# Attention values product: bursts of eight key tiles instead of four, twelve probability buffers, a smaller GpSimd DMA scratch

## The chip, the cores and the metric

The kernel runs on one core of one Trainium2 chip. The metric is the device time of one execution in microseconds (us), the median of several runs. The engines are named as in the profile: PE is TensorE (PEld its weight loads), DVE is VectorE, ACT is ScalarE, POOL is GpSimd, SP is SyncE, which issues the DMA transfers here.

## The reference

One layer is normalised once and then goes two ways, attention over a sliding window and a gating MLP:

```
xn = layernorm(x)                              # x: 2048 x 640
q, k, v = split(xn @ wqkv)                     # 32 heads of width 20
scores = q k^T / sqrt(20), kept where 0 <= query - key < 256
s = concat(softmax(scores) v) @ wo
r = relu(xn @ w1 + b1)                         # 640 -> 1536
g = silu(r * r @ w2 + b2)                      # 1536 -> 640
out = x + s * g
```

All tensors are float32. The window of 256 means that a tile of 128 keys is seen by three tiles of 128 queries: its own and the next two.

## The kernel before, in words

A first stage (to about 140 us of the span) normalises x, transposes it, and makes v for all heads and q, k for the first heads. Products that need the full precision are split into a high and a low part and run as three matmuls.

The middle stage, from about 140 to 770 us, is a loop of 267 steps (`steps`, line 1199). Heads are taken in pairs: 16 pairs `p` (`NP`), each with 16 tiles of queries or keys (`NT`). Step `s` does this, each part for another tile:

- `scores` (line 471): scores of query tile `s`, one matmul for each head of the pair, written to two PSUM tiles `sps`. The pool `pat` holds two such tiles, so the two of the next step reuse those of this one. `maxima` (line 483) has DVE take the row maxima of each.
- `scores_t` (line 512): transposed scores of the key tile nine steps back (`LAG`), both heads, in one PSUM tile `stps` of two banks, of which there is a single one (`ptp`). `exps` (line 523) has ACT write exp of it to a probability tile `p32`, on which POOL zeroes what the mask excludes.
- Every fourth step `max_rows` (line 489) transposes the maxima through columns 384 to 447 of the `stps` tile.
- `fill` (line 1202) puts matmuls of other work, the filler, into the PE queue: q and k of the later heads and the two MLP layers.
- `values` (line 533) is run two steps after the exp of its last key tile (`PLAG`), once in four steps, for four key tiles: the products of the probabilities with v, accumulated in one PSUM bank `ot` (named ops in the profile). The bank has four columns of 128; the outputs of query tile `t` go to column `t // 2 % 4`, and to one of four groups of 32 rows by head and by the parity of `t`. So query tiles 0 and 1 share the rows and column 0 with query tiles 8 and 9. After the burst, ACT copies the two columns that are complete to `osb` (line 552), which goes to DRAM.

PE works in two ways. For all but `values` the array is cut into two halves of 64 rows, and two streams of matmuls run side by side, one per half (`ahead`, `behind`, `both`, lines 438 to 461; the second stream trails the first a little). In `values` all 128 rows are used and the array is cut into four groups of 32 columns. A change between the two is called a turn here.

The order of each engine's work is the order in which the program emits it (a manual schedule). The emission follows a plan: `clock` holds planned times of the two streams, every matmul adds its cost from `COST` (us, line 42), and a burst adds `PV` (1.57) to both. A step has `pace` of planned time (line 1200), the sum of all planned work over the number of steps. In each step, the scores come first, then filler up to 0.4 of the step (`EARLY_FILL`, line 258), then, in a step with a burst, filler up to `PV` before the step's end and the burst, else filler to the step's end:

```
            fill((s + EARLY_FILL) * pace)
            ...
            if e and e[1] % 4 == 3:
                fill((s + 1) * pace - PV)
                values(e[0], e[1] // 4)
            else:
                fill((s + 1) * pace)
```

`fill` emits nothing when the planned clock is past its argument. Other engines' work (`later`, line 583) is emitted once the planned clock has passed its due time; that check is in `fill` too.

The last stage, from about 770 us, is the projection with wo, the gate and the stores.

Of the kernel before, what the change touches and what calls it, by code (L numbers as in the profile page):

```python
# [9 lines left out]
F32 = mybir.dt.float32  # L10
F32R = mybir.dt.float32r
BF16 = mybir.dt.bfloat16
AF = mybir.ActivationFunctionType
ALU = mybir.AluOpType

P = 128
S = 2048
D = 640
# [3 lines left out]
NT = S // P  # L22
KC = D // P
NP = H // 2
NB = 4
BT = S // NB
# [4 lines left out]
HALF = D // 2  # L31
NFH = F // 2 // P
WIDE = 2
FHALF = F // 2
MT = 256
# [5 lines left out]
WARM2 = 10  # L41
COST = {P: 0.067, 2 * P: 0.12, HALF: 0.147, 3 * P: 0.172, BT: 0.23}
SCALE = DH ** -0.5
PV = 1.57
PLAG = 2
NEG = -1.0e30
EPS = 1e-5
SETTLE = 0.45
# [10 lines left out]
def attn_mlp_kernel(ctx: ExitStack, tc, x, wqkv, wo, w1, b1, w2, b2, out):  # L59
    nc = tc.nc  # L60
# [25 lines left out]
    o_d = [dram.tile([NP, P, MT], F32, name=f"o_{g}") for g in range(NB)]  # L86
# [8 lines left out]

    nc.gpsimd.affine_select(mask[:, 0:P], mask[:, 0:P], pattern=[[1, P]], compare_op=ALU.is_gt, fill=NEG, base=0, channel_multiplier=-1)
    nc.gpsimd.affine_select(mask[:, 2 * P:], mask[:, 2 * P:], pattern=[[-1, P]], compare_op=ALU.is_ge, fill=NEG, base=0, channel_multiplier=1)
    mts = [const.tile([P, HP], F32, name=f"mt{j}") for j in range(2)]
# [314 lines left out]
    at2 = ctx.enter_context(tc.tile_pool(name="at2", bufs=2))  # L413
# [4 lines left out]
    def load_v(p):  # L418
        vp = at2.tile([P, NB, 4, 2, VW], F32, tag="vp", name=f"vp_{p}")
        nc.sync.dma_start(vp.rearrange("p b t h w -> p (b t h w)"), v_d[:, p].rearrange("p b n -> p (b n)"))  # L420
        vps[p] = vp

    clock = [0.0, 0.0, 0.0]
# [85 lines left out]
    def pair_tile():  # L509
        return ptp.tile([P, 2, BT], F32, tag="st", name="stps")  # L510
# [10 lines left out]
        return tps, n  # L521

    def exps(p, kb, tps, n):
        p32 = at2.tile([P, 2, 3 * P], F32, tag="p32", bufs=8, name="p32")
        nc.scalar.activation(p32[:, :, :n], tps[:, :, :n], AF.Exp, scale=SCALE)  # L525
        nc.gpsimd.affine_select(p32[:, :, 0:P], p32[:, :, 0:P], pattern=[[0, 2], [1, P]], compare_op=ALU.is_ge, fill=0.0, base=0, channel_multiplier=-1)  # L526
        if n == 3 * P:
            nc.gpsimd.affine_select(p32[:, :, 2 * P:], p32[:, :, 2 * P:], pattern=[[0, 2], [-1, P]], compare_op=ALU.is_gt, fill=0.0, base=0, channel_multiplier=1)  # L528
        pts[p, kb] = p32

    ot = po_.tile([P, 4, P], F32, tag="o", name="ops")

    def values(p, g):
        for kb in range(4 * g, 4 * g + 4):
            pt = pts.pop((p, kb))
            ts = range(kb, min(kb + 3, NT))
            same, other = [t for t in ts if t % 2 == kb % 2], [t for t in ts if t % 2 != kb % 2]
            parts = [same] if kb % 8 < 6 else [[t] for t in same]
            for part in parts + [other]:
                for hh in range(2):  # L540
                    if not part:
                        continue
                    t = part[0]
                    r0 = 32 * (2 * hh + t % 2)
                    c0 = t // 2 % 4
                    first = t % 8 < 2 and kb == max(0, t - 2) or kb == 0
                    nc.tensor.matmul(ot[r0:r0 + VW, c0:c0 + len(part), :], vps[p][:, kb // 4, kb % 4, hh, :], pt[:, hh, :].rearrange("p (t n) -> p t n", n=P)[:, t - kb:part[-1] - kb + 1:2, :], start=first, stop=part[0] == kb, skip_group_check=True)  # L547
        clock[:2] = [max(clock[:2]) + PV] * 2

        def evac():  # L550
            osb = at2.tile([P, 2, P], F32, tag="osb", name="osb")
            nc.scalar.activation(osb, ot[:, 2 * g % 4:2 * g % 4 + 2, :], AF.Copy)
            post(o_d[g][p], osb.rearrange("p e n -> p (e n)"), 0.8)
        later(SOON, evac)


# [4 lines left out]
    def post(dst, src, wait=0.0, then=lambda: None):  # L561
        def go():
            posts.append((dst, src))
            then()
        if whole[0] or not wait:
            go()
        else:
            later(wait, go)

    def post_all():  # L570
        for dst, src in posts:
            nc.sync.dma_start(dst, src)
        posts.clear()
# [9 lines left out]
    def later(wait, fn):  # L583
        tasks.append((clock[0] + wait, len(tasks), fn))

    def soon():
        while tasks:
            first = min(tasks)
            if first[0] > clock[0]:
                return  # L590
            tasks.remove(first)
            first[2]()
# [104 lines left out]
    def ensure_bulk(items):  # L697
        for it in items:
            if it in bulk:
                bulk.remove(it)  # L700
                it[1]()
# [345 lines left out]
    def stored(g):  # L1047
        return NP * NT - NT + 4 * g + 3 + LAG + PLAG

# [19 lines left out]

    def room_of(tag, name):  # L1070
        if tag == "p32":
            return at2.tile([P, 2, 3 * P], F32, tag="p32", bufs=8, name=name).rearrange("p a n -> p (a n)")[:, :D]
        return wgt.tile([P, D], F32, tag=tag, name=name)

    ybt = {}
# [3 lines left out]
    def fetch_y():  # L1079
        if y_early and (1, y_early[0][0]) in stored_y and (y_early[0][2] == 0 or whole[0]):  # L1080
            t, w, i, k = y_early.pop(0)
            if not k:
                y_room.append((at, at1)[i].tile([P, S], F32, tag=f"{w}s{i}", name=f"y{w}{i}"))
            slot = y_room[-1][:, k * D:(k + 1) * D]
            nc.sync.dma_start(slot, y_d[1][:, t, :])
            ybt[t] = slot
# [110 lines left out]

    fl = filler()
    steps = NP * NT + LAG + PLAG
    pace = (8 * (KC - 1) * 15 * COST[BT] + 2 * NB * (15 * (WIDE * COST[BT] + 2 * (NFH - WIDE) * COST[MT]) + 8 * 18 * COST[HALF]) + NP * (2 * NT * COST[3 * P] + NB * PV)) / (steps - 1)  # L1200

    def fill(upto):
        soon()
        while clock[0] < upto:
            c = next(fl, None)
            if c is None:
                clock[0] = upto
                soon()
                return
            if whole[0]:  # L1210
                clock[:2] = [clock[0] + c] * 2
            soon()

    with tc.manual_schedule(engines={E_.PE, E_.Activation, E_.DVE, E_.Pool, E_.SP}):
        load_v(0)
        nc.vector.memset(ot, 0.0)
        loads = []

        def at_step(n):
            return divmod(n, NT) if 0 <= n < NP * NT else None  # L1220

        for s in range(steps):
            state[2] = s
            vload[0] = 0.2 * (s % 4 == 0) + 0.5 * (s % 4 == 3)
            post_all()
            invert()
            if s >= NP * NT - NT + LAG + 2:
                fetch_y()
            issue(RATE)
            a, b, e = (at_step(s - lag) for lag in (0, LAG, LAG + PLAG))  # L1230
            if a:
                p, q = a
                if q == 0:
                    ensure_bulk(loads)
                if s == 2:
                    ones_rows(1)
                if q == 2 and p < NP - 1:
                    assert made_for(p + 1, 0)
                    loads = [bulk_dma(0.7, *l) for l in pair_loads(p + 1, 0)]
                if q == LAG and p < NP - 1:  # L1240
                    assert made_for(p + 1, 1)
                    loads += [bulk_dma(0.7, *l) for l in pair_loads(p + 1, 1)]
                if q == LAG + 4 and p < NP - 1:
                    load_v(p + 1)
            rows = None
            if a:
                sc = scores(p, q)
            if b:
                stp = scores_t(*b)
            if s % 4 == 0 and 0 < s <= NP * NT:  # L1250
                rows = max_rows((s - 1) // NT, (s - 1) % NT // 4, stp[0] if b else pair_tile())
            if a:
                maxima(*a, *sc)
            if b:
                exps(*b, *stp)
            if rows:
                rows()
            fill((s + EARLY_FILL) * pace)
            post_all()
            issue(RATE)  # L1260
            flush()
            tick()
            if e and e[1] % 4 == 3:
                fill((s + 1) * pace - PV)
                values(e[0], e[1] // 4)
            else:
                fill((s + 1) * pace)
        finish()
        post_all()
        state[2] = 10 ** 6  # L1270
        for _ in fl:
            post_all()
            flush(mark() - 1)
        flush()
        post_all()
# [23 lines left out]
```

## Time and profile before

| | |
|---|---|
| median of 3 runs | 851.1 us (851.03 to 851.38) |
| span of the profiled execution, first to last instruction | 849.5 us (the profile lists no other time of this execution) |
| mean granted clock of TensorE | 0.999 |
| PE busy | 841.8 us, 10160 matmuls |
| DVE, ACT, POOL busy | 457.9, 420.9, 330.4 us |
| matmuls of `values` | 2112 instructions in 64 bursts, from 151.8 to 767.7 us |
| copies of their results by ACT | 64 of 378 ns |
| DMA, share of 16 engines (q1, issued by SP) | 63.9%, 164.64 MB |

A busy time is the time in which at least one instruction of the engine runs; those of PE overlap one another. A row of the timeline gives the start, the duration, the engine, the line, the operation, what it writes and reads, the shapes and, in square brackets, how long the engine had been idle and what released it. A float32 matmul of `values` is two instructions in the profile.

### The profile page before, as it was taken

The numbers are of one execution on the slowest core, as the hardware profiler recorded it, in microseconds if no ns is written. First come the engines' busy times: TensorE is split into PE (matmuls) and PEld (weight loads), VectorE is DVE, ScalarE is ACT, GpSimd is POOL, SyncE is SP. The second block draws the span as 40 slices with busy tenths as digits, with TensorE's granted clock in tenths as the row PEclk, the third lists the DMA queues.
The fourth block names the chain that finished last, engine by engine and source line by source line (L and its number), as shares of the span: only waits on it lengthen the run. The fifth ranks groups of instructions, "written<-read, shape, count | busy, mean of one in ns | idle before, by whom it ended". The sixth has DMA issues, their size and how long they took to land.

```text
span 849.5 us, 25542 instructions
## 1 busy us (share of the span) xinstructions
PE 841.8 (99%) x10160; PEld 784.3 (92%) x10160; DVE 457.9 (54%) x1370; ACT 420.9 (50%) x792; POOL 330.4 (39%) x652
## 2 busy tenths in 40 slices
PE   9999999999999999999999999999999999999997
PEld 8999999888888999999999999999999999999997
DVE  7653126665567645455445466755455455436753
ACT  5232114545556763664653664853763754763321
POOL 6010002434334553553552553643553543542442
PEclk9999999999999999999999999999999999999999
DMA  7997587868979565337248245576456355467993
GB/s 248 316 403 286 176 207 260 268 215 266 309 246 288 152 196 151 93 116 200 79 151 219 86 126 151 141 224 188 111 163 199 109 166 190 129 155 212 291 233 118
DMA packets 94398, 166.42 MB, mean 196 GB/s; under 512 B 10952, under 2 KB 43848, under 8 KB 93256
## 3 DMA queue, kind: packets, MB, share of 16 engines
q1 hardware_dynamic: 94120, 164.64, 63.9%
q8 instruction: 80, 1.31, 0.7%
q14 instruction: 38, 0.31, 0.1%
q10 hardware_dynamic: 160, 0.16, 0.1%
HBM read 93.66 MB, written 70.52 MB: 193 GB/s over the span
## 4 chain that ended last, share of the span: by engine, by line
PE 97%; DVE 1%; DMA 1%; issue 0%; ACT 0%; SPq 0%; DVEq 0%
PE yps L469 21%; PE hps L469 21%; PE qkps L469 14%; PE ops L547 10%; PE wops L607 8%; PE vps L229 8%; PE stps L519 5%; PE sps L479 4%; PE qkps L206 3%; PE tps L173 1%; DMA qs<-q_d 0%; DMA xt<-in_A_x_dram 0%; PE tps L302 0%; PE stps L494 0%; PE warm_ps L316 0%
## 5 line engine op out<-in xcount | busy, mean ns | idle before, releaser
L487 DVE CUSTOM_DVE_ANT_0 junk<-sps,mask 128x384 bf16<-128x384 f32 (+2 forms) x512 | 272.6, 532 | 257.7 <-PE hps L469 73.4
L525 ACT ACTIVATE p<-stps 128x768 f32<-128x768 f32 (+2 forms) x256 | 197.4, 771 | 257.2 <-PE stps L519 209.8
L526 POOL TENSOR_SCALAR_AFFINE_SELECT p<-p 128x256 f32<-128x256 f32 x256 | 110.1, 430 | 322.3 <-ACT p L525 317.0
L469 PE MATMUL yps<-w,hh 64*128 64x320 f32 x1536 | 228.3, 310 | 0.8 <-DVE ysb L996 0.7
L469 PE MATMUL hps<-xb,w 64*128 64x256 f32 (+1 forms) x2100 | 218.6, 305 | 0.0
L469 PEld LDWEIGHTS hps<-xb,w 64*128 64x128 f32 x2100 | 199.2, 187 | 6.2 <-issue 5.1
L469 PEld LDWEIGHTS yps<-w,hh 64*128 64x128 f32 x1536 | 181.9, 185 | 5.9 <-issue 3.4
L469 PE MATMUL yps<-w,hl 64*128 64x320 f32 x768 | 174.1, 309 | 0.0
L479 PE MATMUL sps<-ks,qs 60*128 60x384 f32 (+2 forms) x512 | 142.5, 340 | 0.2 <-DVE mt L487 0.2
L519 PE MATMUL stps<-qs,ks 62*128 62x384 f32 (+2 forms) x512 | 136.0, 330 | 0.1
L469 PEld LDWEIGHTS yps<-w,hl 64*128 64x128 f32 x768 | 113.7, 185 | 1.7 <-issue 1.7
L469 PE MATMUL qkps<-xT,wgkh 64*128 64x512 f32 x320 | 100.4, 395 | 0.0
L469 PE MATMUL qkps<-xT,wgqh 64*128 64x512 f32 x320 | 97.8, 392 | 0.0
L528 POOL TENSOR_SCALAR_AFFINE_SELECT p<-p 128x256 f32<-128x256 f32 x224 | 93.6, 418 | 0.0
L547 PE MATMUL ops<-p,vp 128*21 128x128 f32 (+1 forms) x2112 | 92.8, 313 | 0.0
L519 PEld LDWEIGHTS stps<-qs,ks 62*128 62x128 f32 x512 | 88.2, 187 | 1.3 <-issue 0.4
L479 PEld LDWEIGHTS sps<-ks,qs 60*128 60x128 f32 x512 | 86.2, 185 | 2.3 <-DVE mt L487 0.8
L547 PEld LDWEIGHTS ops<-p,vp 128*21 128x21 f32 x2112 | 65.2, 100 | 23.6 <-issue 11.6
L229 PE MATMUL vps<-wv,xT 128*128 128x320 f32 x480 | 71.5, 308 | 0.0
L229 PEld LDWEIGHTS vps<-wv,xT 128*128 128x128 f32 x480 | 70.5, 188 | 0.1
L966 POOL TENSOR_TENSOR hl<-sq,hh 128x512 fp32r<-128x512 f32 x48 | 62.2, 1297 | 18.9 <-ACT sq L965 18.8
L607 PE MATMUL wops<-wo,oT 128*128 128x320 f32 x384 | 61.6, 309 | 0.0
(104 smaller groups left out, 1165.0 us busy)
## 6 DMA issues: line engine op xcount, KB each, us to landing
ks<-k_d SPq DMA_DIRECT2D x64, 240.0 KB
qs<-q_d SPq DMA_DIRECT2D x64, 240.0 KB
xb<-xs SPq DMA_DIRECT2D x60, 256.0 KB
xs<-xT SPq DMA_DIRECT2D x8, 1280.0 KB
k_d<-shm SPq DMA_DIRECT2D x19, 512.0 KB
q_d<-shm SPq DMA_DIRECT2D x19, 512.0 KB
y<-ysb SPq DMA_DIRECT2D x28, 320.0 KB
o<-osb SPq DMA_DIRECT2D x64, 128.0 KB
```

The costliest lines, as they stand in the source:

```text
L206: nc.tensor.matmul(ps, wt[:, c, :], xT[part][b][:, c * BT + t0:c * BT + t0 + n], start=m == 1, stop=m == 3 * KC)
L229: nc.tensor.matmul(ps, xT[xp][b][:, c * BT + t * P: c * BT + (t + 1) * P], wv[wp][:, c, nh * HALF:(nh + 1) * HALF], start=first and m == 0 ...
L469: return nc.tensor.matmul(out, a[r], b_[r], skip_group_check=True, **kw)
L479: nc.tensor.matmul(ss[hh][:, :nk], qs[i][o, q * P:(q + 1) * P], ks[i][o, k0 * P:k0 * P + nk], start=True, stop=True)
L487: nc.vector.tensor_tensor_reduce(out=junk[:, :nk], in0=ss[hh][:, :nk], in1=mask[:, 3 * P - nk:], scale=1.0, scalar=-3.0e38, op0=ALU.add, o ...
L519: nc.tensor.matmul(tps[:, hh, :n], ks[i][o, kb * P:(kb + 1) * P], qs[i][o, kb * P:kb * P + n], start=True, stop=True)
L525: nc.scalar.activation(p32[:, :, :n], tps[:, :, :n], AF.Exp, scale=SCALE)
L526: nc.gpsimd.affine_select(p32[:, :, 0:P], p32[:, :, 0:P], pattern=[[0, 2], [1, P]], compare_op=ALU.is_ge, fill=0.0, base=0, channel_multip ...
L528: nc.gpsimd.affine_select(p32[:, :, 2 * P:], p32[:, :, 2 * P:], pattern=[[0, 2], [-1, P]], compare_op=ALU.is_gt, fill=0.0, base=0, channel ...
L547: nc.tensor.matmul(ot[r0:r0 + VW, c0:c0 + len(part), :], vps[p][:, kb // 4, kb % 4, hh, :], pt[:, hh, :].rearrange("p (t n) -> p t n", n=P ...
L607: nc.tensor.matmul(ps, a, b_, start=j == 0, stop=j == n - 1)
L966: nc.gpsimd.tensor_sub(hh[1][:, :BT], sq, f32(hh[0]))
```

## The change

`values` takes a range of key tiles in place of a group number. For the first 15 head pairs there are two ranges of eight tiles, for the last pair four of four as before. The planned cost of a burst becomes `TURN + PV * len` with 0.33 and 0.31 us, which is 1.57 for four tiles as before and 2.81 for eight. A burst of eight reaches query tile 8, whose column is that of query tiles 0 and 1; so in the burst, after its second key tile, ACT is given a copy of that one column (`leave`, at `kb % 8 == 1`), and the other three are copied after the burst. The probability tiles go from eight buffers to twelve. The DMA scratch that is set aside for GpSimd shrinks to 2048 bytes per partition.

```diff
-PV = 1.57
+PV = 0.31
+TURN = 0.33
+PBUF = 12
...
-        p32 = at2.tile([P, 2, 3 * P], F32, tag="p32", bufs=8, name="p32")
+        p32 = at2.tile([P, 2, 3 * P], F32, tag="p32", bufs=PBUF, name="p32")
...
-    def values(p, g):
-        for kb in range(4 * g, 4 * g + 4):
+    def bursts(p):
+        return (range(0, 8), range(8, NT)) if p < NP - 1 else [range(4 * g, 4 * g + 4) for g in range(NB)]
+
+    def burst_of(p, kb):
+        return next((r for r in bursts(p) if r[-1] == kb), None)
+
+    def burst_cost(r):
+        return TURN + PV * len(r)
+
+    def values(p, kbs):
+        osbs, out_ = {}, set()
+
+        def leave(g, e):
+            if g not in osbs:
+                osbs[g] = at2.tile([P, 2, P], F32, tag="osb", name="osb")
+            nc.scalar.activation(osbs[g][:, e], ot[:, (2 * g + e.start) % 4:(2 * g + e.start) % 4 + e.stop - e.start, :], AF.Copy)
+
+        for kb in kbs:
             pt = pts.pop((p, kb))
...
-        clock[:2] = [max(clock[:2]) + PV] * 2
+            if kb % 8 == 1 and kb + 6 in kbs:
+                leave(kb // 4, slice(0, 1))
+                out_.add(kb // 4)
+        clock[:2] = [max(clock[:2]) + burst_cost(kbs)] * 2
 
         def evac():
-            osb = at2.tile([P, 2, P], F32, tag="osb", name="osb")
-            nc.scalar.activation(osb, ot[:, 2 * g % 4:2 * g % 4 + 2, :], AF.Copy)
-            post(o_d[g][p], osb.rearrange("p e n -> p (e n)"), 0.8)
+            for g in sorted({kb // 4 for kb in kbs}):
+                leave(g, slice(int(g in out_), 2))
+                post(o_d[g][p], osbs[g].rearrange("p e n -> p (e n)"), 0.8)
...
-    pace = (... + NP * (2 * NT * COST[3 * P] + NB * PV)) / (steps - 1)
+    pace = (... + NP * 2 * NT * COST[3 * P] + sum(burst_cost(r) for p in range(NP) for r in bursts(p))) / (steps - 1)
...
-            if e and e[1] % 4 == 3:
-                fill((s + 1) * pace - PV)
-                values(e[0], e[1] // 4)
+            r = e and burst_of(*e)
+            if r:
+                fill((s + 1) * pace - burst_cost(r))
+                values(e[0], r)
...
-    nc = bacc.Bacc("TRN2", target_bir_lowering=False, num_devices=1)
+    nc = bacc.Bacc("TRN2", target_bir_lowering=False, num_devices=1, dynamic_dma_scratch_size=2048)
```

More of the change, by code (lines that the diff above doesn't have):

```diff
@@ L1071, in room_of @@
         if tag == "p32":
-            return at2.tile([P, 2, 3 * P], F32, tag="p32", bufs=8, name=name).rearrange("p a n -> p (a n)")[:, :D]
+            return at2.tile([P, 2, 3 * P], F32, tag="p32", bufs=PBUF, name=name).rearrange("p a n -> p (a n)")[:, :D]
         return wgt.tile([P, D], F32, tag=tag, name=name)
@@ L1199, in attn_mlp_kernel @@
     steps = NP * NT + LAG + PLAG
-    pace = (8 * (KC - 1) * 15 * COST[BT] + 2 * NB * (15 * (WIDE * COST[BT] + 2 * (NFH - WIDE) * COST[MT]) + 8 * 18 * COST[HALF]) + NP * (2 * NT * COST[3 * P] + NB * PV)) / (steps - 1)
+    pace = (8 * (KC - 1) * 15 * COST[BT] + 2 * NB * (15 * (WIDE * COST[BT] + 2 * (NFH - WIDE) * COST[MT]) + 8 * 18 * COST[HALF]) + NP * 2 * NT * COST[3 * P] + sum(burst_cost(r) for p in range(NP) for r in bursts(p))) / (steps - 1)
     def fill(upto):
```

## The prediction

> **What bounds the kernel now.** I read the profile's page first, then PE's own waits.
>
> ```profile
> span 849.5 us, 25542 instructions
> PE 841.8 (99%) x10160; PEld 784.3 (92%) x10160; DVE 457.9 (54%) x1370; ACT 420.9 (50%) x792; POOL 330.4 (39%) x652
> PE 97%; DVE 1%; DMA 1%; issue 0%; ACT 0%; SPq 0%; DVEq 0%
> ...
> PE warm_ps L269 <- POOL ident L92: 1.7, 1, 1.7
> PE yps L469 <- DVE ysb L996: 0.7, 1, 0.7
> PE sps L479 <- DVE mt L487: 0.2, 1, 0.2
> ```
>
> PE carries 97% of the chain of waits and waits 2.6 us in all. So every us of PE work that goes is a us of time, and every new PE wait is one too: there is no slack on PE to hide it. The plan's clock follows the chip well (below), so the question is what the new burst does to PE's work and to PE's waits.
>
> Next the timeline of PE around two bursts (start, duration):
>
> ```profile
> 307.14 0.34 PE L479 MATMUL sps<-ks,qs 60*128 60x384 f32 x1
> 307.37 0.34 PE L479 MATMUL sps<-ks,qs 60*128 60x384 f32 x1
> ...
> 308.26 1.21 PEld L547 LDWEIGHTS ops<-p,vp 128*21 128x21 f32 x32 [0.19 <-issue]
> 308.26 1.50 PE L547 MATMUL ops<-p,vp 128*21 128x256 f32 x32
> ...
> 309.69 0.18 PEld L469 LDWEIGHTS yps<-w,hh 64*128 64x128 f32 x1 [0.22 <-issue]
> 309.70 0.44 PE L479 MATMUL sps<-ks,qs 60*128 60x384 f32 x1
> ...
> 317.51 0.32 PE L469 MATMUL yps<-w,hl 64*128 64x320 f32 x2
> 317.66 0.45 PE L469 MATMUL yps<-w,hh 64*128 64x320 f32 x3
> 318.04 1.52 PE L547 MATMUL ops<-p,vp 128*21 128x256 f32 x40
> ...
> L547 PE MATMUL ops<-p,vp x32: 272/334/395, 308.3 to 309.5; 128*21 128x256 f32 x16, 128*21 128x128 f32 x16
> ...
> L547 PE MATMUL ops<-p,vp 128*21 128x128 f32 x1344 | 88.6, 274 | 0.0
> L547 PE MATMUL ops<-p,vp 128*21 128x256 f32 x768 | 75.1, 382 | 0.0
> ```
>
> The two bursts start 9.78 us apart, 2.45 us a step. The plan says 2.40: its whole work is 638.7 us (339.7 and 110.4 us of filler, 88.1 of scores, 64 bursts of 1.57), over 266 steps. The burst starts 1.12 us after its step's scores; the plan says 0.4 of a step, 0.96, plus up to one matmul. I rely on that match.
>
> **Turns saved.** 64 bursts become 30 of eight and 4 of four, so 30 pairs of turns go; the matmuls stay. What one pair costs: two row matmuls take 0.15 us (317.51 to 317.66), so the three from 317.66 are worth 0.22, the next could start at 317.88, and the burst starts at 318.04: 0.16 lost on entry. On exit the last weight load ends at 308.26 + 1.21 = 309.47 and the next starts at 309.69: at most 0.22 lost, or nothing if the last matmuls only drain. So 0.16 to 0.38. A middle value comes from the two mean durations: 108 ns more for 128 more columns. The 32 instructions (16 of each form) stream 48 such units over four column groups, 12 x 0.108 = 1.30 us, against 1.43 from burst start to the next row matmul: 0.13 on exit. I take 0.16 + 0.13 = 0.29, 30 times: **-8.7 us** (-4.8 to -11.4).
>
> **The copy inside the burst.** `leave` puts an ACT copy of column 0 behind the second key tile. The third key tile writes columns 1 and 2 of the same bank. Does it wait? The nearest case is the exp in steps with transposed maxima, whose matmuls write columns of the `stps` bank that exp does not read. The timeline of one, and the whole run's waits for that line:
>
> ```profile
> 322.18 0.34 PE L519 MATMUL stps<-qs,ks 62*128 62x384 f32 x1
> 322.36 0.22 PE L494 MATMUL stps<-ident,mt 64*64 64x64 f32 x1
> 322.61 0.81 ACT L525 ACTIVATE p<-stps 128x768 f32<-128x768 f32 x1 [1.09 <-PE stps L494]
> ...
> ACT p L525: 38.7, 44
> ...
> L308 ACT ACTIVATE xT<-tps 128x128 fp32r<-128x128 f32 x4 | 1.1, 270 | 0.0
> L552 ACT ACTIVATE osb<-ops 128x256 f32<-128x256 f32 x64 | 24.2, 378 | 0.0
> ...
> 307.93 0.81 ACT L525 ACTIVATE p<-stps 128x768 f32<-128x768 f32 x1 [0.23 <-PE stps L519]
> 308.64 0.62 ACT L965 ACTIVATE sq<-relu 128x512 f32<-128x512 f32 x1
> ...
> L796 ACT ACTIVATE w<-raw 128x640 fp32r<-128x640 f32 x12 | 8.8, 732 | 0.5 <-DMA raw<-in_B_w_dram 0.5
> ```
>
> Exp starts 0.03 us after the transposes end (322.58), not after the scores it reads (322.52); 44 of its waits go to them. The order is kept for the bank, not for the columns. So I expect the third key tile to wait for the copy.
>
> The Trainium skill agrees in its page "PSUM — Partial Sum Buffer", section "PSUM bank collisions raise a hardware error": two engines on one bank and one quadrant of 32 partitions at a time are an error, whatever the columns, so guard by bank and quadrant, not by address. By that rule this wait comes in all 30 bursts; by addresses alone it would come at the seventh key tile only and cost nothing (the second rival).
>
> Price: the first two key tiles are half of the 32 instructions, so the 16th starts about 0.62 into the burst and ends 0.27 later, at 0.89. The copy starts 0.03 later, lasts 0.27 (the 128-column row of line 308), and PE goes on 0.06 after it (DVE to PE, 248.61 to 248.67 in the rows of the next part): 1.25. Without the copy the third tile would start at 0.65. That is 0.60 lost, with PE idle and everything in its queue behind. Below, 0.36 if the drain costs nothing. Above, 1.3 when a weight split of 0.73 stands ahead on ACT; in the burst above exp and the square keep ACT until 1.00, so the copy is 0.08 late. I take 0.60 + 0.06: **+19.8 us** (+11 to +30; the 1.3 can't hold for all).
>
> **The step after the burst.** Before, the plan's clock stood at 0.96 + 1.57 = 2.53 us after a burst: a step and 0.13. Now the pace is 2.364 (628.8 us over 266), 0.4 of it 0.946, and the burst 2.81: 3.756, that is 1.59 steps. `fill((s + 1) * pace - burst_cost(r))` asks for a time already past and moves nothing earlier. So the scores of step s+1 follow the burst at once, and those of step s+2 come at 4.728, **0.97 us after them**, with only 0.6 us of filler between. Can their readers keep up? The rows after the burst at 308.26, and the one PE wait on DVE that the kernel before has:
>
> ```profile
> 309.98 0.34 PE L519 MATMUL stps<-qs,ks 62*128 62x384 f32 x1
> 310.09 0.34 PE L479 MATMUL sps<-ks,qs 60*128 60x384 f32 x1
> 310.32 0.56 DVE L487 CUSTOM_DVE_ANT_0 junk<-sps,mask 128x384 bf16<-128x384 f32 x1 [1.44 <-PE yps L469]
> 310.64 0.81 ACT L525 ACTIVATE p<-stps 128x768 f32<-128x768 f32 x1 [1.38 <-PE stps L519]
> 311.03 0.56 DVE L487 CUSTOM_DVE_ANT_0 junk<-sps,mask 128x384 bf16<-128x384 f32 x1
> 311.51 0.48 DVE L996 TENSOR_TENSOR ysb<-yps,b2t 128x320 f32<-128x320 f32 x1
> 311.92 0.22 PE L479 MATMUL sps<-ks,qs 60*128 60x128 f32 x1
> ...
> 248.05 0.56 DVE L487 CUSTOM_DVE_ANT_0 junk<-sps,mask 128x384 bf16<-128x384 f32 x1
> 248.11 0.34 PE L479 MATMUL sps<-ks,qs 60*128 60x384 f32 x1
> 248.67 0.44 PE L479 MATMUL sps<-ks,qs 60*128 60x384 f32 x1 [0.18 <-DVE mt L487]
> ```
>
> DVE ends the second maximum at 311.59, 1.90 us after PE left the burst. Its tile can be written 0.06 later, as at 248.67, after the maximum that ended at 248.61. So the second scores of step s+2 can't start before 1.96. The plan puts the first at 0.97 + 0.10 (the first matmul after a turn takes 0.44, not 0.34), the second 0.23 to 0.39 later (307.14 to 307.37, 309.70 to 310.09): 1.30 to 1.46, give or take a matmul of 0.2. At 248.67 nothing passed the waiting matmul. The `stps` tile comes free at 310.64 + 0.81 = 311.45, 1.76 after the turn, so exp hides behind this wait. I take 0.60 (0.3 to 0.85), 30 times: **+18.0 us** (+9 to +25).
>
> What is late next: work due during the burst is emitted in one lump behind the maxima and exp of step s+1, like the ysb at 311.51, and 2.81 us of due times come at once in place of 1.57. The readers of step s+2 can start late and hold step s+3. None of the rows shows such a wait, so it may be nothing; 0.4 would be a lump of one ysb too many. I take 0.07, nearer nothing since step s+3 is a full 2.36 us later: **+2 us** (0 to +12).
>
> **At nothing.** The stores of the copies, in the list of DMA issues:
>
> ```profile
> o<-osb SPq DMA_DIRECT2D x64, 128.0 KB
> ```
>
> Ten probability tiles are live when a burst starts (eight and two ahead) and two more fill before it ends, so twelve suffice and exp never waits; with eight the loop could not run. ACT copies a burst's results in three pieces for two, some 0.16 us more, while ACT is half idle. The same 64 stores leave in pairs. GpSimd's scratch serves DMA that POOL issues, and all issues listed are SP's.
>
> **Sum.** -8.7 + 19.8 + 18.0 + 2 = +31.1 us on the span of 849.5: 880.6. The median of the runs is 1.6 above that span: **882 us**, its own range 868 to 897.
>
> **Rivals.**
> - *Only the wait on DVE.* The order on the bank goes by columns; the copy, over at 1.25, is needed at the seventh key tile, at about 6 x 0.32 = 1.95. Against it stands exp behind the transposes. 882 - 20 = 862 us.
> - *Only the copy.* The scores of step s+2 come late enough, because the plan runs behind the chip there. It needs 0.6 us more filler between the two steps than the plan puts; the 1.12 us before the burst speak against it. 882 - 20 = 862 us.
> - *Faster: the waits are passed by.* PE takes up later matmuls while one waits, so that filler covers both waits and only the turns count: 851.1 - 8.7 = 842 us. It decides once it covers 31 of the 40 us. The rows at 248.11 and 248.67 are against it: PE stood idle with filler queued.
> - *Worse: lumps.* DVE or ACT still busy at step s+3 add 0.5 to 0.8 us a burst: 900 us. The kernel before spreads this work without waits, but over shorter bursts.
>
> **How the numbers follow.** Both waits 0.74; only DVE 0.10; only the copy 0.07; passed by 0.05; lumps 0.04. The time is that of the first, 882. The range takes in the two cases at 862 and its own upper bound: 860 to 897. A difference under 0.2% can't be told from none here. Faster 0.05, same 0.02, slower 0.93.
>
> **What would show it.** In the profile after: 34 bursts, the long ones 3.4 us with a gap of 0.6 behind the second key tile, released by ACT's copy; `sps` waiting on DVE's `mt` some 30 times, 0.5 to 0.7 us each; PE's share down to 95%. The turns show as bursts fewer by 30 with the same 2112 matmuls. I am wrong if the third key tile starts while the copy runs, if the two scores of steps s+1 and s+2 lie more than 2 us apart without a wait, or if PE is still 99% busy.

## The result and the profile after

The changed kernel takes **898.2 us** (897.9 to 898.6) against 851.2 before: 1.0549 times as long, 95% interval 1.0534 to 1.0564. Slower was forecast, at 882 with a range to 897; the time lies 1.2 us above that range, and the loss is 47 us where 31 were worked out.

The page of the changed kernel, span, busy engines and the chain of waits, and then PE's own waits (engine and line, what it waited for: us in all, times, longest):

```profile
span 896.9 us, 25566 instructions
PE 854.4 (95%) x10160; PEld 797.4 (89%) x10160; DVE 457.2 (51%) x1370; ACT 427.6 (48%) x822; POOL 332.1 (37%) x652
PE 84%; DVE 5%; DMA 3%; ACT 3%; issue 2%; SPq 1%; POOL 1%; DVEq 0%
...
PE ops L565 <- ACT osb L550: 12.0, 22, 1.0
PE sps L481 <- DVE mt L489: 8.6, 32, 0.3
PE yps L471 <- DVE ysb L1017: 8.3, 3, 7.2
PE ops L565 <- POOL p L530: 3.6, 7, 0.5
```

PE does the same 10160 matmuls, but its share is 95%, and its part of the chain fell from 97% to 84%. Three waits stand out where the kernel before had almost none. (The view counts a wait from the drawn end of the matmul before it; by the starts of the matmuls, as used below, PE stands still for longer.)

The timeline of the first long burst and the step after it, in chosen rows:

```profile
161.04 0.85 PE L565 MATMUL ops<-p,vp 128*21 128x256 f32 x16
161.60 0.59 ACT L906 ACTIVATE shm<-qkps 128x512 fp32r<-128x512 f32 x1
162.08 0.28 ACT L550 ACTIVATE osb<-ops 128x128 f32<-128x128 f32 x1
162.50 2.17 PE L565 MATMUL ops<-p,vp 128*21 128x256 f32 x56 [0.61 <-ACT osb L550]
164.60 0.44 PE L481 MATMUL sps<-ks,qs 60*128 60x384 f32 x1
164.94 0.34 PE L481 MATMUL sps<-ks,qs 60*128 60x384 f32 x1
165.17 0.56 DVE L489 CUSTOM_DVE_ANT_0 junk<-sps,mask 128x384 bf16<-128x384 f32 x1 [2.61 <-PE qkps L471]
165.79 0.44 PE L481 MATMUL sps<-ks,qs 60*128 60x384 f32 x1
165.88 0.56 DVE L489 CUSTOM_DVE_ANT_0 junk<-sps,mask 128x384 bf16<-128x384 f32 x1
166.50 0.44 PE L481 MATMUL sps<-ks,qs 60*128 60x384 f32 x1 [0.27 <-DVE mt L489]
```

The burst breaks after its 16th instruction, two key tiles in, and goes on only after ACT's copy of column 0 (162.08 to 162.36), which itself stood behind another ACT task. Then the scores of step s+1 start at 164.60, those of step s+2 already at 165.79, and the second of these waits until the maximum that starts at 165.88 has ended at 166.44: 1.90 after the burst. Both start 0.06 us after a maximum ends (the first ends at 165.73), so both waited for DVE. Over all 30 long bursts the trace has this break at the 16th instruction, and the second scores of step s+2 start 0.71 us after the first on average, where the median before was 0.24.

The third wait comes once, in the last stage (chosen rows):

```profile
798.73 0.58 SPq L1129 DMA_DIRECT2D sums<-rec  x1
801.90 1.18 SPq L1085 DMA_DIRECT2D rec<-o  x2
805.43 1.56 DVE L1144 TENSOR_TENSOR ob<-ob,sums 128x512 f32<-128x512 f32 x2 [6.02 <-DMA rec<-o]
809.86 0.95 DVE L1087 RECIPROCAL rec<-rec 128x128 f32<-128x128 f32 x1 [2.87 <-DMA rec<-o]
810.73 0.43 DVE L1017 TENSOR_TENSOR ysb<-yps,yin 128x320 f32<-128x320 f32 x1
811.21 0.90 PE L471 MATMUL yps<-w,hh 64*128 64x320 f32 x4 [7.17 <-DVE ysb L1017]
```

DVE, in order, waits for two loads; the evacuation of an MLP bank stands behind them, and PE behind that, for 7.2 us. The wait costs more than that. By the trace the granted clock of TensorE is 0.5 from 806.7 to 817.0 us, so PE goes on at half rate after it: six MLP matmuls take 0.80 us (812.18 to 812.98) where they took 0.44 (795.24 to 795.68). The 40 that start between 811.2 and 817.0 take 2.9 us more than at the rate before. The page's line of the granted clock (40 slices of the span, in tenths) and rows before and after the wait:

```profile
PEclk9999999999999999999999999999999999997999
...
795.24 0.46 PE L471 MATMUL yps<-w,hh 64*128 64x320 f32 x4
...
795.68 0.46 PE L471 MATMUL yps<-w,hh 64*128 64x320 f32 x4
...
812.18 0.73 PE L471 MATMUL yps<-w,hh 64*128 64x320 f32 x4
...
812.98 0.73 PE L471 MATMUL yps<-w,hh 64*128 64x320 f32 x4
```

So this one wait is worth about 10.1 us (an estimate from these rows).

### The profile page after: what moved, and what is told of

Same layout as the page of the kernel before. It is cut to its first block, busy times and chain, and to the rows that moved or that the text cites. A ratio compares the mean times of both kernels' runs of the same rounds, so it can differ in the third digit from the quotient of the medians.

```text
span 896.9 us, 25566 instructions
## 1 busy us (share of the span) xinstructions
PE 854.4 (95%) x10160; PEld 797.4 (89%) x10160; DVE 457.2 (51%) x1370; ACT 427.6 (48%) x822; POOL 332.1 (37%) x652
## 4 chain that ended last, share of the span: by engine, by line
PE 84%; DVE 5%; DMA 3%; ACT 3%; issue 2%; SPq 1%; POOL 1%; DVEq 0%
PE yps L471 18%; PE hps L471 18%; PE qkps L471 11%; PE wops L628 8%; PE ops L565 8%; PE vps L231 8%; PE sps L481 5%; PE stps L521 4%; DVE junk L489 4%; PE qkps L208 3%; DMA raw<-in_A_wqkv_dram 1%; ACT p L527 1%; DMA rec<-o 1%; PE tps L175 1%; DMA qs<-q_d 1%
## 5 line engine op out<-in xcount | busy, mean ns | idle before, releaser
L471 PE MATMUL hps<-xb,w 64*128 64x256 f32 (+1 forms) x2100 | 210.9, 305 | 0.4 <-DVE ysb L1017 0.4
L471 PEld LDWEIGHTS yps<-w,hh 64*128 64x128 f32 x1536 | 188.3, 187 | 14.2 <-DVE ysb L1017 10.0
L471 PEld LDWEIGHTS hps<-xb,w 64*128 64x128 f32 x2100 | 195.0, 187 | 3.8 <-issue 2.5
L471 PE MATMUL yps<-w,hl 64*128 64x320 f32 x768 | 180.3, 311 | 0.0
L481 PE MATMUL sps<-ks,qs 60*128 60x384 f32 (+2 forms) x512 | 136.8, 347 | 8.7 <-DVE mt L489 8.6
L521 PE MATMUL stps<-qs,ks 62*128 62x384 f32 (+2 forms) x512 | 125.7, 337 | 0.0
L471 PEld LDWEIGHTS yps<-w,hl 64*128 64x128 f32 x768 | 123.6, 187 | 0.7 <-issue 0.6
L481 PEld LDWEIGHTS sps<-ks,qs 60*128 60x128 f32 x512 | 79.4, 185 | 20.9 <-DVE mt L489 19.6
L521 PEld LDWEIGHTS stps<-qs,ks 62*128 62x128 f32 x512 | 77.9, 187 | 0.7 <-ACT p L527 0.5
L471 PE MATMUL qkps<-xT,wgkl 64*128 64x512 f32 x160 | 62.1, 394 | 0.0
```

The source lines that it names most:

```text
L471: return nc.tensor.matmul(out, a[r], b_[r], skip_group_check=True, **kw)
L481: nc.tensor.matmul(ss[hh][:, :nk], qs[i][o, q * P:(q + 1) * P], ks[i][o, k0 * P:k0 * P + nk], start=True, stop=True)
L521: nc.tensor.matmul(tps[:, hh, :n], ks[i][o, kb * P:(kb + 1) * P], qs[i][o, kb * P:kb * P + n], start=True, stop=True)
```

## The experiments

All times are medians; each ratio is to the kernel before on the same chip.

**No copy inside the burst.** `leave` at `kb % 8 == 1` goes, and so that no sum is zero the start flag is set at key tile 0 alone:

```diff
-                    first = t % 8 < 2 and kb == max(0, t - 2) or kb == 0
+                    first = kb == 0
...
-            if kb % 8 == 1 and kb + 6 in kbs:
-                leave(kb // 4, slice(0, 1))
-                out_.add(kb // 4)
```

> The changed kernel without the copy inside the burst: all four columns are copied after it, and the start flag is set at key tile 0 alone, so that query tiles 8 and on are added onto those before; the output is wrong by that, the matmuls are as many. Theory 1 (the copy holds PE in each of the 30 long bursts, 22 us in the trace of the changed kernel): 876 us, bursts of 72 and 60 matmuls as long as 2.83 and 2.5 us, the waits of the next scores on DVE still there. Theory 2 (the wait only uncovers another one behind it, masks of POOL or a late exp, at the same place): over 888 us. Theory 3 (the long burst itself is slow, the columns stream worse in a row of eight): the bursts stay over 3.2 us and the time near 898.

877.35 us, ratio 1.0304 (1.0287 to 1.0321): the copy costs **20.9 us**, 0.70 a burst. The burst at 161 us and PE's waits in that run:

```profile
L565 PE MATMUL ops<-p,vp x72: 272/273/396, 161.1 to 163.6; 128*21 128x128 f32 x48, 128*21 128x256 f32 x24
...
PE yps L471 <- DVE ysb L1014: 8.9, 3, 7.8
PE sps L481 <- DVE mt L489: 8.4, 31, 0.3
```

The 72 instructions start within 2.5 us, in the changed kernel within 3.4. No wait on POOL or on ACT is left in the bursts, so theory 2 falls: the waits put down to POOL after the copy were the same stop. Theory 3 falls too. The waits on DVE are untouched.

**Scores apart.** In each step without a burst, the last `fill` goes on until the next scores are 2.05 us behind this step's in the plan:

```diff
+            began = clock[0]
             if a:
                 sc = scores(p, q)
...
-                fill((s + 1) * pace)
+                fill(max((s + 1) * pace, began + APART))
```

> The changed kernel with one more rule in the plan: the scores of two steps are planned at least 2.05 us apart, so the step after a long burst gets more filler and the next three give it back. Theory 1 (30 waits on DVE of about 0.55 us cost 17 us): 881 us, no scores waiting on DVE's maxima. Theory 2 (the lump of work that is emitted behind the burst is what holds PE): the wait moves to a later step and the time stays over 892.

871.33 us, ratio 1.0229 (1.0214 to 1.0244): **26.9 us** less than the changed kernel, more than either theory gave. PE's longest waits are then:

```profile
PE ops L566 <- ACT osb L551: 11.9, 22, 1.1
PE yps L472 <- DVE ysb L1018: 6.2, 3, 5.6
PE ops L566 <- POOL p L531: 3.8, 7, 0.8
```

`sps` waiting on `mt` is gone from the list, and the scores of step s+2 start 2.25 us after those of s+1, where it was 1.21. The late second scores (0.71 less 0.24) and the late first ones (1.21 against a planned 1.07) make 0.61 a burst, 18 us. That is less than the wait costs. In 28 of the 30 steps s+2 no matmul starts on either half between the first and the second scores, so that in 0.71 us PE takes up one matmul of a planned 0.17 on one half; and after the second, with one matmul of the other half beside it, the next starts 0.28 us later, where with the scores apart three start within 0.19. Counted as the time from scores to scores, less the burst and the planned cost of the matmuls in it, steps s+1 and s+2 have 32.9 us left over in the changed kernel and 7.1 with the scores apart: 25.8 us, 0.86 a burst (an estimate, since the costs are the plan's; the two profiled executions lie 29.0 us apart). Some 1.6 us more are the shorter wait near the end.

**Both.**

> Both edits at once, output wrong as in the run without the copy. Theory 1 (two separate waits): both gains add up, 898 - 22 - 17 = 859 us, and what is left over 842 (before less the turns) is the wait of 7 us near the end and some small ones. Theory 2 (the two waits cover one another): over 868.

848.67 us, ratio 0.997 (0.9957 to 0.9983). 49.5 us go, and the two single gains add up to 47.8: two separate waits. It is above the 842 of the prediction's "passed by" case by 6.7. The wait near the end makes up more than that, with 5.9 us and some 2.0 more at a granted clock of 0.5 behind it:

```profile
PE yps L472 <- DVE ysb L1015: 6.5, 3, 5.9
```

**Buffers and scratch alone**, put into the kernel before (`bufs=12`, `dynamic_dma_scratch_size=2048`).

> The kernel before with twelve probability buffers and the GpSimd scratch of 2048 bytes, nothing else. Theory 1 (both cost nothing): 851 us, within 0.2%. Rival (the moved buffers or the scratch slow something): over 853.

852.06 us, ratio 1.0009 (0.9999 to 1.0018): no difference that can be told from none.

**Six key tiles.** Six tiles touch eight query tiles, which just fill the four columns, so no copy stands inside a burst; after each burst ACT copies the columns that are complete:

```diff
-        return (range(0, 8), range(8, NT)) if p < NP - 1 else ...
+        return (range(0, 6), range(6, 12), range(12, NT)) if p < NP - 1 else ...
```

> Bursts of six, six and four key tiles: query tiles 0 to 7 fill the four columns, so no copy stands inside a burst. 49 bursts in place of 64, planned cost 2.19 for six. The plan overshoots: 0.946 + 2.19 = 3.14, so the second next scores are planned 1.6 us after the next. Theory 1 (a wait on DVE until 1.96 after the turn, bounds as measured with eight: planned 1.7 to 1.9 for the second scores): 30 waits of 0.1 to 0.3 us eat the 15 turns (4.2 us): 848 to 856. Rival (the waits come with any long burst): over 860.

855.56 us, ratio 1.0052 (1.0036 to 1.0069). The time lies in the range of theory 1, but not for its reason: the scores of step s+2 start 1.67 us after those of s+1 and the second 0.27 later, and PE's list has no wait on DVE's maxima. So with eight it is not the long burst as such but how far the plan overshoots, as the run with the scores apart shows too. PE's longest wait here is one of 2.0 us on `ysb` near the end; what else keeps the saved turns from showing is not known.

**Six and apart.**

> Bursts of six, six and four, and scores planned at least 2.05 us apart. Theory 1: no copy inside a burst, no wait on DVE, 15 turns of 0.28 us saved: 847 us, faster than both kernels, unless the wait near the end (6 us) comes here too: then 853. Rival (turns are worth nothing): 851 without that wait.

857.28 us, ratio 1.0067 (1.0054 to 1.0079): both theories missed. There was no wait that spacing could cure, and two waits of the transposed scores for the row maxima's transfer came in:

```profile
PE stps L522 <- DMA qs<-mrow: 3.9, 2, 2.3
PE yps L472 <- DVE ysb L1015: 2.6, 2, 2.2
```

**The wait near the end, first idea:** the loads of the sums (`rec<-o`) stand behind those of the output rows (`ob<-o`) in SP's queue. One step earlier:

```diff
-            if not over and state[2] < stored(g) + 3:
+            if not over and state[2] < stored(g) + 2:
```

> The changed kernel with the loads of the sums for the reciprocals one step earlier (two steps after the last burst of a group in place of three). Theory 1 (the wait of 7 us at 811 us comes from the order of two loads: the rows for the output before the sums, so that the reciprocal stands in DVE's queue ahead of an evacuation that PE needs): 891 us, no PE wait over 2 us. Rival (the loads are just slow there, or another work holds DVE): still 898 and a wait of several us.

897.79 us, ratio 1.0546 (1.053 to 1.0562); the wait is still 5.3 us. The sums are now loaded first (793.6 us, the output rows from 798.1), and DVE stands for 7.1 us at the product that waits for the output rows instead. So the order of the two loads decides 1.9 us of the wait and nothing that shows in the time. With six key tiles the same edit told nothing more:

> Bursts of six, six and four, scores planned apart and the loads of the sums one step earlier. Theory 1: 847 us with or without a wait near the end in the run before. Rival (the order of these loads does not matter): as the run with six and apart.

859.2 us, ratio 1.0081 (1.0063 to 1.0099).

**Second idea:** the filler runs out. MLP matmuls that run after the start of the last burst: first the kernel before (last burst at 766.7 us), then the run below with the lower pace (805.8); in the changed kernel (820.8) there are none.

```profile
L469 PE MATMUL yps<-w,hh 64*128 64x320 f32 x34 | 5.9, 312 | 0.1
L469 PE MATMUL yps<-w,hl 64*128 64x320 f32 x19 | 4.9, 311 | 0.0
```

```profile
L471 PE MATMUL yps<-w,hh 64*128 64x320 f32 x46 | 7.7, 313 | 0.0
...
L471 PE MATMUL yps<-w,hl 64*128 64x320 f32 x23 | 5.9, 306 | 0.0
```

The edit takes a little planned time from each step, so that the steps are done earlier and filler is left:

```diff
+    pace -= 0.0135
```

> The changed kernel with 0.0135 us less planned time a step, so that some 3.5 us of filler are left when the last burst starts, as in the kernel before (in the changed kernel none is left). Theory 1 (the wait of 7 us near the end comes since the filler runs out before the last steps, and the chain of loads, sums and evacuations of the last stage lies bare): that wait under 1 us, 891 us. Rival (it comes from the order or the speed of the loads): the wait stays over 4 us, 897.

892.95 us, ratio 1.0484 (1.047 to 1.0497): 5.3 us less, PE's longest wait on `ysb` is 1.5 us, and the granted clock stays at 1 until the end of the span. The wait and the slow clock behind it were worth about 10.1; where the rest went is not known. The same with neither copy nor bunched scores:

> Without the copy inside the burst (output wrong: query tiles 8 and on are added onto those before), scores planned apart, and the lower pace. Theory 1: only the saved turns are left, 851.3 - 8 = 843 us. Rival: the wait at the end stays: 848.

851.61 us, ratio 0.9996 (0.9986 to 1.0007): a miss. The long wait is gone, but the time is some 3 us longer than with both edits at the old pace. Shorter waits have come, which do not add up to all that was lost:

```profile
PE yps L472 <- DVE ysb L1015: 2.1, 3, 1.0
PE stps L522 <- DMA qs<-mrow: 1.4, 1, 1.4
PE yps L472 <- ACT relu L980: 1.2, 2, 0.6
PE sps L482 <- DVE mt L490: 1.0, 3, 0.4
```

So I shifted the pace of the kernel before, with bursts of four, up (`pace += 0.0135`) and down (`pace -= 0.008`):

> The kernel before, bursts of four, with 0.0135 us more planned time a step: the filler is used up earlier, and none should be left at the last burst, as in the changed kernel. Theory 1 (the filler that runs out lays the last stage's chain bare): a PE wait of several us near the end, 855 to 858 us. Rival (that wait needs the long bursts): 851, no such wait.

864.0 us, ratio 1.0148 (1.0122 to 1.0173). No MLP matmul starts after the last burst, and PE waits:

```profile
PE wops L607 <- DVE res L1187: 4.1, 1, 4.1
PE yps L469 <- DVE ysb L996: 3.7, 2, 3.5
PE stps L519 <- DMA qs<-mrow: 1.8, 2, 1.2
```

The wait on `ysb` near the end comes without any long burst. It was 3.5 us here and 7.2 in the changed kernel. The total went past what was expected, by a second wait in the projection and by the clock: after each of the two the granted clock is 0.5 for some us, which adds 2.8 and 1.6. With the waits that is 12.0 of the 12.6 us.

> The kernel before with 0.008 us less planned time a step, the same edit as in the runs with six key tiles. Theory 1 (those gained by the turns saved): 851.4, no gain from the pace alone. Rival (the pace is what gained): 849.5.

859.9 us, ratio 1.0093 (1.0076 to 1.011): both theories missed. A pace 0.3% lower costs the kernel before 8.5 us, 2.9 of them in one wait of `wops` on `res` and 1.6 in the slow clock after it; the rest is not placed here. The pace before sits at a point from which either step loses.

All the profiles together fit the idea that the filler left at the last burst decides the wait of `yps` on `ysb` near the end. Where none is left (five runs with eight key tiles, and the kernel before at the higher pace), PE waits 3.5 to 7.8 us; where 31 matmuls are left (six key tiles at the full pace), 2.0 to 3.1; where 53 or more are left, at most 1.5.

**Six key tiles at the lower pace** (`pace -= 0.008`), without and with scores kept 1.9 us apart:

> Bursts of six, six and four with 0.008 us less planned time a step. Theory 1: the wait of 2.2 us near the end goes, 853 us or a little less. Rival: 855.6 as without it.

849.48 us, ratio **0.9977** (0.9969 to 0.9986): faster than both kernels, by 0.23% over the one before, and faster than either theory had it (853 and 855.6). Its only PE waits past the start:

```profile
PE yps L471 <- ACT relu L979: 0.5, 1, 0.5
PE sps L481 <- DVE mt L489: 0.4, 1, 0.4
```

> Bursts of six, six and four, scores planned 1.9 us apart, 0.008 us less planned time a step. Theory 1: no wait on DVE, none near the end, 15 turns saved: 848 us. Rival (spacing the scores delays the row maxima and their transfer, on which the transposed scores then wait, as 3.9 us did with 2.05): 853 to 857.

849.71 us, ratio 0.9981 (0.9969 to 0.9993): the same within the intervals. Of the two forecasts theory 1 (848) was nearer. The lower pace alone made bursts of four slower, so it alone does not explain the gain of six key tiles.

## Why the prediction was right or wrong

- *Direction: right*, by the two waits it named, both where it put them.
- *Turns, -8.7 us.* From burst start to the next row matmul all bursts together took 88.3 us before and 84.5 in the run without the copy: 3.8 on exit (0.13 each). On entry a burst of the kernel before starts 0.26 us after the last row matmul, on average, which is 0.09 more than that matmul's planned cost; the prediction's rows gave 0.16. With 0.09 to 0.16 (an estimate) that is 6.5 to 8.6, under the 8.7 but near it. The Trainium skill, page "TensorEngine Tiling (Array Packing)", section "Tiling Modes", says that a change of tiling mode drains TensorE, without a price; these runs give 0.22 to 0.29 us for the two changes of a burst.
- *Copy, +19.8 us: right*, 20.9 measured. The order is kept for the whole bank, as read from exp behind the transposes (or for the tile that fills the bank: the runs don't tell these apart); the rival with the wait on DVE alone, which had it go by columns, is out. The Trainium skill's rule in "PSUM — Partial Sum Buffer", section "PSUM bank collisions raise a hardware error", to guard by bank and not by address, is kept here: in all 30 bursts PE stops after the 16th instruction, not at the seventh key tile. No run lets two engines meet on the bank, so the error itself is not shown.
- *A first step that failed, the size of "Scores of step s+2", +18.0 us (+9 to +25).* The place and the wait were right: they came 1.21 us after those of s+1, the second at 1.92 (1.96 worked out). But the term took only how late the second scores start. It left out that meanwhile nothing starts on the other half either, and that after the wait the next start is 0.28 us away. The two steps after a burst lose 25.8 us by it, 0.86 a burst in place of 0.60, and spacing the scores saved 26.9.
- *The other step that failed: "What is late next".* It looked one step ahead only, at DVE and ACT, and gave 2 us, 0 to 12. At step s+3, where it looked, there is next to nothing (0.08 us a burst over the planned costs, 0.04 with the scores apart). The wait near the end was not in it: 7.2 us, and some 2.9 more at the granted clock of 0.5 behind it. The working took the plan's total as kept and did not ask how much filler is left when the last steps come. The rows for it were there: 53 MLP matmuls after the last burst at 766.7 us. In the changed kernel none is left, and the MLP evacuations come to stand in DVE's queue behind work of the last stage that still waits for its loads. That a lack of filler brings such a wait is shown by the run of the kernel before at the higher pace, and that its cure helps by the changed kernel at the lower one (5.3 us). Why the filler is ahead by that much was not tested. It goes with the number of bursts (53 matmuls left with 64 bursts, 31 with 49, none with 34), and the code offers a cause: each burst sets both planned streams to the later of the two, a loss that `pace` does not count.
- *Waits passed by (842): out.* In all 30 stops in a burst and in 28 of the 30 stops before the second scores, no later matmul started. *Only the copy*, or *only the wait on DVE* (862 each): out, since each wait alone is worth over 20 us. *Worse: lumps* (900) came nearest to the measured time, but by luck: its wait at step s+3 is not there.
- *At nothing: right* for buffers and scratch (0.9999 to 1.0018). (The full list of DMA issues has two of ACT's beside SP's, and none of POOL's.)

Put together: without the copy and with the scores apart 49.5 us go, and what is left is 2.6 under the kernel before, since the saved turns and the wait near the end nearly cancel. That is the 47 us. Against the 31 worked out, the scores are some 8 us dearer and the wait near the end adds some 10, while the lumps are next to nothing.

## What to carry to other kernels

Here a longer burst would have saved its turn only with nothing put inside it: a copy out of the bank that the burst is writing stops TensorE for the copy and both handovers, here more than two turns. When a planned piece is longer than the gap it is put in, look at the step after it: work that was spaced by the plan comes in a bunch, and a buffer with one reader sets how close it may come. In a schedule that is written out, also count what filler is left for the last steps, since there a shift of 0.3% of the pace cost as much (8.5 us) as the saved turns were worth.

## What was not expected of the hardware

The turn into the 32-column groups and back costs 0.22 to 0.29 us together, while a 128 x 128 ACT copy of 0.28 us between two matmuls on one bank costs TensorE 0.70. A long wait of PE costs more than its length: in these profiles each one in the loop or later of 2.9 us or more (up to 7.8) has a granted clock of 0.5 for 3.4 to 10.2 us around or after its end; of the three from 2.2 to 2.7 us two have it, and those of 2.0 and less don't. And the kernel's time is not smooth in the plan: 0.0135 us a step more or 0.008 less cost 12.6 and 8.5 us with bursts of four, while 0.008 less gained 6.1 with bursts of six (855.6 to 849.5).
